# Third batch's k and q also through DMA transposes, two plain heads per row, attention stores on GpSimd's queue

## The chip, the cores and the metric

The kernel runs on one core of one Trainium2 chip. The metric is device time in microseconds (us) of one execution. The kernel before the change takes 313.95 us, the median of 13 runs that lie between 311.17 and 316.79 us.

## The reference

Dilated and plain sliding-window attention on 8 batches, 8 heads, 576 positions and head size 64, then a feed-forward layer with SiLU on the 4608 tokens. Inputs and output are float32; the kernel computes in float16 with float32 accumulation.

```python
scores = scale * np.matmul(q, k.transpose(0, 1, 3, 2))
rel = pos[:, None] - pos[None, :]
mask_plain = (rel >= 0) & (rel < 32)                       # heads 0 to 3
mask_dil = (rel >= 0) & (rel < 128) & (rel % 4 == 0)       # heads 4 to 7
attn = softmax(where(mask, scores, -1e9));  o = attn @ v
x = o.transpose(0, 2, 1, 3).reshape(4608, 512)
h = x @ w_in                                               # 512 x 2048
out = (h * sigmoid(h)) @ w_out                             # 2048 x 512
```

## The kernel before, in words

**Feed-forward.** Tokens go in groups: two of 256, then eight of 512. A group has 16 first-layer tiles `h` (line 892, 4 matmuls each: weights `w_in`, moving operand x transposed, 512 or 256 columns). ScalarE takes the tanh of a tile (line 901) and VectorE makes `gT = (th + 1) * h` of it (line 903). The second layer (line 925) makes an output tile `y` of 128 tokens by 16 matmuls of 512 columns, in four steps of 4; step n reads the n-th quarter of `w_out`. ScalarE copies it out (line 938) and its queue stores it.

**Attention.** Of each batch the first four heads are "plain", the last four "dilated" (positions split in 4 residues). A batch's score work is cut in sets (`S`, lines 605 to 650): matmuls of transposed k and q (line 632), exp on ScalarE, a mask product on VectorE. The products with v (`P` plain, `D` dilated, line 677) are divided by their sums on VectorE (lines 680 and 681) into `oP` and `oD`.

**Two ways to transposed k and q.** Batches below `PEB` (0, 1 and 2) take the PE path: k and q are loaded with positions on partitions (`nat`, `issue_nat`, line 124, GpSimd's queue) and transposed on TensorE against an identity: `TD` for dilated heads (line 544), `TA` and `TB` for plain ones (lines 521 and 535), these after VectorE has put two heads side by side (`paired`, `N`, line 656). The results are copied out of PSUM by VectorE or ScalarE (lines 510 and 512). Batches 3 to 7 take the DMA path: `issue_cast` (line 141) copies k and q to DRAM in float16 (`kq_s`), and `issue_turn` loads them by DMA transposes from SyncE's queue, n = 0 and 1 for plain k and q (line 155, into the `nat` buffers), n = 2 and 3 for dilated k and q (line 158, into `kqT`). The plain transpose reads 2304 rows of 128 elements at a step of 64, so that each row holds a position and the next one.

**Attention's output.** Of batches 0 to 2, `oP` and `oD` are transposed on TensorE into `xA` (`XP`, `XD`). From batch 3 on they are stored to DRAM (`x_s`, lines 696 and 715, SyncE's queue: two stores of `oP`, two of `oD` for each batch) and come back transposed by DMA for each group (line 450, SyncE's queue).

**What sets the order.** The code is written out as one program in which each engine runs its instructions in the order written. At build time a planner (`Plan`, `Step`) picks the next piece of TensorE work from three lists (attention of each batch in an order written out by hand, first-layer tiles, second-layer steps) by estimated costs and due times. The loads of the start are issued in the order of `ORDER` with the costs `LOAD_US`. DMA-path work is written where the planner believes its inputs to be there: `loads_gen(b)` (line 424) first writes "fence" copies on GpSimd, which wait for the dilated transposes of the batch before (line 427) and for the x transpose of an earlier group (line 429), then v's two loads (lines 165 and 178) and the cast of batch b; `turn_gen(b)` (line 410) writes the four transposes; `stored(b)` starts `group_gen` (line 447) once four stores of a batch are written. The number of buffers is two for `nat`, `kqT` and v, three for x in flight.

**The start.** Eight matmuls of 512 columns on zeros (line 192) keep TensorE busy before data is there. Batch 0 has its own, finer transposes (`TD`, `TR`, `TA`, `TS`).

Of the kernel before, what the change touches and what calls it, by code (L numbers as in the profile page):

```python
# [16 lines left out]
def kernel(  # L17
# [32 lines left out]
    PEB = 3  # L50
# [5 lines left out]
    ORDER = "k0 r0 w0b v0 w0a w1 w2 w3 d1 p1 o0 r1 o1 o2 o3 v1".split()  # L56
    LOAD_US = {"w": 2.57, "o": 2.57, "d": 3.2, "p": 3.0, "r": 2.3, "v": 2.57, "k0": 2.2, "r0": 1.0, "v0": 2.3, "w0a": 1.3, "w0b": 1.3}
    AT_W0 = 11.4
# [32 lines left out]
    NW = HN * S  # L91
# [47 lines left out]
    def issue_cast(b):  # L139
        for i, src in enumerate((k, q)):  # L140
            nc.gpsimd.dma_start(
                out=kq_s[b][i].rearrange("(n p c) -> p n c", c=512, p=144),
                in_=src[b].rearrange("h s d -> (h s d)").rearrange("(n p c) -> p n c", c=512, p=144),
            )

    def issue_turn(b, n):
        i = n % 2
        flat = kq_s[b][i]
        if n < 2:
            if b < PEB + 2 and i == 0:  # L150
                nc.gpsimd.memset(kq_plain(b)[0][:, :LEAD], 0.0)
            win = bass.AP(tensor=flat.tensor, offset=flat.offset, ap=[[D, NW], [1, P]])
            dst = kq_plain(b)[i]
            dst = dst[:, LEAD:] if i == 0 else dst
            nc.sync.dma_start_transpose(out=dst[:, None, :], in_=win)
        else:
            rows = flat[HN * S * D :].rearrange("(n c) -> n c", c=DIL * D)
            nc.sync.dma_start_transpose(out=kqTs[b % 2][:, i], in_=rows)
# [29 lines left out]
    warm = vraws[1].rearrange("p a h r d -> p (a h r d)")  # L188
    nc.vector.memset(warm[:, :GT], 0.0)
    y_warm = ps_y.tile([P, GT], F32, tag="y", name="y_warm")  # L190
    for n in range(8):
        nc.tensor.matmul(y_warm, warm[:, :P], warm[:, :GT], start=True, stop=True)
    nc.vector.memset(warm[:, GT:], 0.0)
# [67 lines left out]
    def third_batch():  # L261
        for n in range(2, PEB):
            issue_nat(n, 0, H)
        issue_vraw(2)
        issue_vp(2)
        issue_cast(PEB)
        yield "DMA", 0.0
# [12 lines left out]
    class Plan:  # L280
        def __init__(self):
            self.t = 0.0
            self.now = 0.0
            self.mode = 128
            self.free = {"ACT": 5.7, "DVE": 6.6}
            self.heap = []
            self.n = 0
            self.rings = {nm: [] for nm in RINGS}
# [72 lines left out]
    AT_DIL = {0: 6.1, 1: AT["d1"], 2: t2 + 7.0}  # L361
    AT_PLAIN = {0: 9.3, 1: AT["p1"], 2: t2 + 7.0}
    AT_VRAW = {0: 10.1, 1: AT["r1"], 2: t2 + 8.6}
    AT_VP = {0: 11.4, 1: AT["v1"], 2: t2 + 11.4}
    AT_CAST = t2 + 18.0
# [37 lines left out]
    turned = {b: Step(None, 0.0) for b in range(PEB, B)}  # L403
# [6 lines left out]
    def turn_gen(b):  # L410
        for n, us in enumerate((3.0, 3.0, 1.5, 7.5)):
            issue_turn(b, n)
            yield "DMA", us
        for n in (b, b + 1) if b == 3 == PEB else (b + 1,):
            if n < B:
                count(("L", n), loads_need(n), lambda n=n: start_loads(n))
# [4 lines left out]
    def start_turn(b):  # L421
        plan.push(turned[b], turn_gen(b), plan.now)

    def loads_gen(b):
        last = max(b - 1, PEB)
        for i in range(2):
            nc.gpsimd.tensor_copy(fence[:, i : i + 1], kqTs[last % 2][:, i, 1, HN * M - 1 :])  # L427
        if b - 2 >= PEX:
            nc.gpsimd.tensor_copy(fence[:, 2:3], x_of(first_of[b - 2])[:, HP - 1, GT - 1 :])
        issue_vraw(b)  # L430
        issue_vp(b)
        if b > PEB:
            issue_cast(b)
        yield "DMA", 9.0
        v_in[b].done = plan.now
        if b > PEB:
            yield "DMA", 4.5
            count(("T", b), 2, lambda: start_turn(b))
# [8 lines left out]
    def group_gen(g):  # L447
        t0 = max(GROUPS[g][0], PEX * S)
        n = sum(GROUPS[g]) - t0
        nc.sync.dma_start_transpose(  # L450
            out=x_of(g)[:, :, GT - n :], in_=x_s[t0 : t0 + n]
        )
        yield "DMA", 6.0
        b = need[g]
        if g == first_of[b] and b + 2 < B:
            count(("L", b + 2), loads_need(b + 2), lambda: start_loads(b + 2))

# [8 lines left out]
    def attention(b):  # L466
# [21 lines left out]
        def k_plain(i, hp, j):  # L488
            r = slice(i * D, i * D + D)
            if pe_path:  # L490
                return kP[r, hp, QB * j : QB * j + P]
            c = LEAD + (2 * hp + i) * S + QB * j - W - i
            return kW[r, c : c + P]

        def q_plain(i, hp, j):
            r = slice(i * D, i * D + D)
            if pe_path:
                return qP[r, hp, QB * j : QB * (j + 1)]
            c = (2 * hp + i) * S + QB * j - i
            return qW[r, c : c + QB]  # L500
# [184 lines left out]
        def av_p(ring, j):  # L685
            def lhs(i):
                return prob_cols(("p", j, i // 2), i % 2)

            yield from av(
                ring, f"p{j}", oP[:, j], rcps[:, j], lhs, lambda i: vp[:, i * NB + j, : D + 1]  # L690
            )
            parts[j // 3] += 1
            if not pe_x and parts[j // 3] == 3:
                j = j // 3 * 3 + 2
                rows = x_s[b * S : (b + 1) * S, : HN * D].rearrange("(j p) c -> p j c", p=QB)
                nc.sync.dma_start(
                    out=rows[:, j - 2 : j + 1],
                    in_=oP[:, j - 2 : j + 1].rearrange("p j h d -> p j (h d)"),
                )
                yield "DMA", 3.0  # L700
                stored(b)

        def av_d(ring, ab, r):
# [8 lines left out]
            if not pe_x and parts[2 + ab] == DIL:  # L712
                t0 = b * S + ab * DIL * MH
                rows = x_s[t0 : t0 + DIL * MH, HN * D :].rearrange("(m r) c -> m r c", r=DIL)
                nc.sync.dma_start(out=rows, in_=oD[:, ab].rearrange("p r h d -> p r (h d)"))
                yield "DMA", 3.0
                stored(b)
# [24 lines left out]
        if b == 0:  # L742
            order = [
                ("TA", 1, "q"), ("TA", 0, "q"), ("V", 0), ("TD", 3), ("TS", 1), ("TS", 0),
                ("TD", 0), ("TA", 0, "k"), ("TD", 2), ("TD", 1), ("TA", 1, "k"), ("S", 3),
                ("TR",), ("S", 4), ("S", 6), ("S", 0), ("S", 1), ("D", 0, 1), ("P", 1), ("S", 5),
                ("D", 0, 0), ("D", 0, 2), ("V", 1), ("P", 0), ("S", 2), ("P", 3), ("P", 2),
                ("D", 1, 1), ("P", 4), ("D", 0, 3), ("P", 5), ("XP", 0), ("XP", 1), ("D", 1, 2),
                ("XD", 0), ("D", 1, 0), ("XP", 4), ("D", 1, 3), ("XP", 5), ("XP", 2), ("XD", 1),
                ("XP", 3), ("M",), ("B",),  # L750
            ]
        elif pe_path:
            order = [
                ("N", "k"), ("TD", 3), ("TD", 0), ("TD", 2), ("V", 0), ("TD", 1), ("N", "rest"),
                ("TA", 1), ("N", "q"), ("S", 3), ("TA", 0), ("TB", 0), ("TB", 1), ("D", 0, 1),
                ("D", 0, 0), ("S", 4), ("D", 0, 2), ("S", 0), ("P", 1), ("S", 1), ("D", 0, 3),
                ("P", 2), ("P", 0), ("XP", 0), ("XP", 1), ("S", 5), ("S", 6), ("XD", 0), ("V", 1),
                ("D", 1, 3), ("XP", 2), ("S", 2), ("D", 1, 2), ("D", 1, 0), ("D", 1, 1), ("P", 3),
                ("XP", 3), ("P", 4), ("XD", 1), ("P", 5), ("XP", 4), ("XP", 5),
            ]  # L760
        else:
            order = [
                ("S", 2), ("S", 0), ("P", 1), ("S", 3), ("S", 4), ("S", 1), ("S", 5), ("P", 0),
                ("V", 0), ("P", 5), ("P", 3), ("D", 0, 3), ("V", 1), ("P", 4), ("P", 2),
                ("D", 1, 1), ("D", 1, 3), ("D", 0, 1), ("D", 0, 2), ("D", 1, 2), ("D", 1, 0),
                ("D", 0, 0),
            ]
            if pe_x:
                order.insert(order.index(("D", 0, 0)), ("XP", 0))
                order.insert(order.index(("D", 0, 0)), ("XP", 1))  # L770
                order.insert(order.index(("D", 0, 2)), ("XP", 2))
                order.insert(order.index(("D", 0, 2)), ("XP", 3))
                order.insert(order.index(("D", 1, 0)), ("XP", 4))
                order.insert(order.index(("D", 1, 0)), ("XP", 5))
                order += [("XD", 0), ("XD", 1)]
        for key in order:
# [9 lines left out]
            elif kind == "TA" and b == 0:  # L786
                st = Step(
                    lambda ring, a=a: trans_a0(ring, *a), 0.36, rings,
                    [AT_PLAIN[0]],
# [18 lines left out]
            elif kind == "S":  # L808
                if not pe_path:
                    deps = [turned[b]]  # L810
# [170 lines left out]
    LOOK = 8  # L981
    LIM_ATT = 1.1
    LIM_PAIR = 0.4
    LIM_L1 = 1.8
    SIDE = 0.9
    NEAR = 1.0
    SPARE = 6
    seconds = {st.mate for _, st in att if st.mate}
    side = 0.0
    while att or l1 or l2:  # L990
# [12 lines left out]
        if l2:  # L1003
            main.append((l2, l2[0], 9.0))
        cands = main + cands if side > SIDE else cands + main
# [21 lines left out]
        if pick is None:  # L1027
            waits += [plan.heap[0][0]] if plan.heap else []
# [39 lines left out]
```

The softmax here doesn't subtract the row's maximum and nothing guards it: scores larger than these inputs give would overflow.

## Time and profile before

| what | value |
|---|---|
| median of 13 runs (lowest, highest) | 313.95 us (311.17, 316.79) |
| the profiled execution's own time | 311.17 us |
| its span, first to last instruction | 309.4 us |
| TensorE busy with matmuls | 299.0 us, 97% of the span |
| weight loads, VectorE, ScalarE, GpSimd | 155.5, 196.2, 164.5, 54.7 us |
| bytes moved by DMA | 44.55 MB in 107382 packets |
| first-layer and second-layer matmuls | 640 and 592 |
| first `h` matmul starts | 22.03 us |
| last attention matmul | 231.3 us |

The page of the profile gives busy time by engine, then the span in 40 slices with the busy share in tenths, then the DMA queues, the chain of work that ended last, groups of instructions by line, and DMA issues. A matmul's end is modelled, and a busy TensorE may still run below its peak; start-to-start times say more. Further answers of the trace give waits, order of time by engine, and sums over stretches of time. In instruction groups the row is: line, engine, operation, out<-in, count, busy us, mean ns, idle before it and what ended that.

### The profile page before, as it was taken

The numbers are of one execution on the slowest core, as the hardware profiler recorded it, in microseconds if no ns is written. First come the engines' busy times: TensorE is split into PE (matmuls) and PEld (weight loads), VectorE is DVE, ScalarE is ACT, GpSimd is POOL, SyncE is SP. The second block draws the span as 40 slices with busy tenths as digits, with TensorE's granted clock in tenths as the row PEclk, the third lists the DMA queues.
The fourth block names the chain that finished last, engine by engine and source line by source line (L and its number), as shares of the span: only waits on it lengthen the run. The fifth ranks groups of instructions, "written<-read, shape, count | busy, mean of one in ns | idle before, by whom it ended". The sixth has DMA issues, their size and how long they took to land.

```text
span 309.4 us, 6177 instructions
## 1 busy us (share of the span) xinstructions
PE 299.0 (97%) x2402; PEld 155.5 (50%) x2402; DVE 196.2 (63%) x498; ACT 164.5 (53%) x318; POOL 54.7 (18%) x86
## 2 busy tenths in 40 slices
PE   7789989999999999999999999999999999999995
PEld 3468755555545544554455444544454444444444
DVE  6399998699868735794589457854794355355000
ACT  7478872667573626454663456436643445455111
POOL 8855723001900005000600050000000000000000
PEclk9999999999999999999999999999999999999999
DMA  8999999998999949999999999974115400000222
GB/s 104 184 199 197 195 190 206 204 190 164 141 193 217 181 124 151 217 185 188 134 212 216 200 144 209 231 157 108 38 56 144 98 36 34 34 34 2 79 91 71
DMA packets 107382, 44.55 MB, mean 144 GB/s; under 512 B 73304, under 2 KB 102872, under 8 KB 107352
## 3 DMA queue, kind: packets, MB, share of 16 engines
q0 software_dynamic: 48528, 19.86, 52.6%
q1 hardware_dynamic: 53496, 14.91, 25.3%
q10 hardware_dynamic: 5328, 9.37, 8.8%
q8 instruction: 19, 0.31, 0.4%
q14 instruction: 11, 0.09, 0.1%
HBM read 39.81 MB, written 18.28 MB: 188 GB/s over the span
## 4 chain that ended last, share of the span: by engine, by line
PE 87%; DVE 5%; ACT 3%; DMA 2%; issue 1%; POOL 1%; ACTq 0%; DVEq 0%; POOLq 0%
PE y L925 40%; PE h L892 37%; PE s L632 3%; PE av_d L677 3%; DMA nat<-in_q_dram 2%; PE av_p L677 2%; DVE probs L650 1%; DVE oD L681 1%; ACT probs L641 1%; ACT ob L938 1%; ACT kqD L510 1%; PE s L620 1%; DVE oP L681 1%; DVE gT L903 1%; POOL nat L131 1%
## 5 line engine op out<-in xcount | busy, mean ns | idle before, releaser
L925 PE MATMUL y<-w_out,gT 128*128 128x512 f16 (+1 forms) x592 | 137.8, 373 | 0.0
L901 ACT ACTIVATE th<-h 128x512 f32<-128x512 f32 (+1 forms) x160 | 88.9, 557 | 78.3 <-PE h L892 68.8
L903 DVE SCALAR_TENSOR_TENSOR gT<-th,h 128x512 f16<-128x512 f32 (+1 forms) x160 | 99.2, 628 | 47.7 <-ACT th L901 47.2
L892 PEld LDWEIGHTS <-w_in 128*128 128x128 f16 x640 | 59.0, 97 | 52.3 <-issue 1.2
L925 PEld LDWEIGHTS <-gT 128*128 128x128 f16 x592 | 55.1, 98 | 57.5
L892 PE MATMUL h<-xR,w_in 128*128 128x512 f16 x320 | 77.6, 379 | 0.0
L892 PE MATMUL h<-xA,w_in 128*128 128x512 f16 (+1 forms) x320 | 62.0, 336 | 0.0
L938 ACT ACTIVATE ob<-y 128x512 f32<-128x512 f32 (+1 forms) x36 | 21.3, 591 | 42.6 <-PE y L925 42.6
L641 ACT ACTIVATE probs<-s 128x768 f16<-128x768 f32 (+2 forms) x32 | 24.7, 772 | 11.8 <-PE s L632 10.0
L677 PEld LDWEIGHTS <-probs 128*128 128x128 f16 x448 | 21.9, 98 | 16.1 <-DVE probs L650 3.0
L681 DVE TENSOR_TENSOR oD<-av_d,rcps 72x256 f16<-72x256 f32 x64 | 26.9, 421 | 2.2
L650 DVE TENSOR_TENSOR probs<-probs,mask_p 128x768 f16<-128x768 f16 x21 | 11.5, 551 | 22.6 <-ACT probs L641 22.6
L681 DVE TENSOR_TENSOR oP<-av_p,rcps 96x256 f16<-96x256 f32 x48 | 20.2, 421 | 1.6
L427 POOL COPY fence<-kqT 128x1 f16<-128x1 f16 x10 | 2.3, 232 | 95.7 <-DMA kqT<-kq_s 95.7
L645 ACT ACTIVATE probs<-s 128x384 f16<-128x384 f32 (+2 forms) x38 | 17.2, 479 | 1.0 <-PE s L632 1.0
L677 PE MATMUL av_d<-vd,probs 128*128 128x65 f16 x256 | 15.2, 194 | 1.3 <-DVE oD L681 0.6
L945 DVE TENSOR_SCALAR ob<-y 128x128 f32<-128x128 f32 x1 | 0.3, 290 | 20.6 <-ACT ob L943 20.6
L677 PE MATMUL av_p<-vp,probs 128*128 128x65 f16 x192 | 12.0, 194 | 0.3
L680 DVE RECIPROCAL rcps<-av_d 72x4 f32<-72x4 f32 x64 | 11.0, 172 | 2.0 <-PE av_d L677 1.9
L165 POOL DMA_DIRECT2D vraw<-in_v_dram x16 | 10.8, 677 | 5.6 <-DVE gT L903 2.2
L650 DVE TENSOR_TENSOR probs<-probs,mask_d 128x576 f16<-128x576 f16 (+1 forms) x23 | 11.6, 512 | 0.0
L680 DVE RECIPROCAL rcps<-av_p 96x4 f32<-96x4 f32 x48 | 8.3, 172 | 5.2 <-PE av_p L677 5.2
(93 smaller groups left out, 155.9 us busy)
## 6 DMA issues: line engine op xcount, KB each, us to landing
out_dram<-ob ACTq DMA_DIRECT2D x35, 256.0 KB, 2.9
kq_s<-in_k_dram POOLq DMA_DIRECT2D x5, 576.0 KB, 8.9
kq_s<-in_q_dram POOLq DMA_DIRECT2D x5, 576.0 KB, 10.9
vp<-in_v_dram POOLq DMA_DIRECT2D x7, 384.0 KB, 7.4
w_out<-in_moe_w_out_dram POOLq DMA_DIRECT2D x4, 512.0 KB, 10.5
vraw<-in_v_dram POOLq DMA_DIRECT2D x8, 224.0 KB, 5.2
w_in<-in_moe_w_in_dram POOLq DMA_DIRECT2D x3, 512.0 KB, 9.6
x_s<-oP SPq DMA_DIRECT2D x10, 144.0 KB, 3.3
```

The lines of the kernel that those rows point to most:

```text
L165: nc.gpsimd.dma_start(out=vraw[p0 : p0 + m1 - m0, ab].rearrange("p h r d -> p h (r d)"), in_=src[m0:m1],)
L641: nc.scalar.activation(p2, both[:, :, :n], AF.Exp, scale=scale)
L645: nc.scalar.activation(p2[:, i], sp[i][:, :n], AF.Exp, scale=scale)
L650: nc.vector.tensor_tensor(p2, p2, mk, ALU.mult)
L677: nc.tensor.matmul(a[:, i, : D + 1], lhs(i), rhs(i), start=True, stop=True)
L680: nc.vector.reciprocal(rcp[:n], a[:n, :, D : D + 1])
L681: nc.vector.tensor_tensor(o, a[:n, :, :D], rcp[:n, :, None].broadcast_to([n, HN, D]), ALU.mult)
L892: nc.tensor.matmul(h[:, :w], w_in16[:, c, f * P : (f + 1) * P], x_g[:, c], start=(c == 0), stop=(c == HP - 1),)
L901: nc.scalar.activation(th[:, :w], h[:, :w], AF.Tanh, scale=0.5)
L903: nc.vector.scalar_tensor_tensor(gTs[g][:, f, :w], th[:, :w], 1.0, h[:, :w], ALU.add, ALU.mult)
L925: nc.tensor.matmul(y, gTs[g][:, f, tb * P : (tb + 1) * P], w_out16[:, f, c0:c1], start=(f == 0), stop=(f == NFF - 1),)
L938: nc.scalar.activation(ob, y, AF.Copy, scale=0.5)
```

## The change

- `PEB` goes from 3 to 2: batch 2 takes the DMA path. Its outputs still go through TensorE (`PEX` stays 3).
- `issue_cast` writes plain heads two by two: DRAM rows of 128 elements with both heads' 64 at one position. For that it issues, for each of k and q, two copies of 1152 runs of 64 elements and one copy of the dilated heads; six DMAs for a batch where there were two.
- `issue_turn` reads 1152 such rows for plain k and for plain q, where there were 2304.
- Stores of `oP` and `oD` go from SyncE's queue to GpSimd's, in the order in which the planner lets them.
- The fence copy on x (line 429) is gone.
- Start loads are reordered: half of batch 1's k and q (`p1`) ahead of `w_in`, `o1` ahead of `o0`; the cast of batch 2 follows instead of its `nat` loads and precedes its v.
- Nine warming matmuls of 512 columns at the start, and up to 18 us of planned time fillers of 128 columns wherever the planner finds nothing to do (80 in the program).
- Attention's hand-written orders, the planner's limits and its estimates are new. Plain and dilated transposes have due times of their own (`turned["p", b]`, `turned["d", b]`).

In the program order that results, TensorE's list loses 48 transposes of batch 2 (24 `TD`, 16 `TA`, 8 `TB`) and gains 1 + 80 warming matmuls. SyncE's list, from batch 4 on, is: two plain transposes of batch b; the x transpose of an earlier group; two dilated ones of batch b (in batches 6 and 7 the x transpose follows the dilated ones). GpSimd's list of a batch: two fences, three v loads, six casts, then four stores of the batch before it.

```diff
-    PEB = 3
+    PEB = 2
-    ORDER = "k0 r0 w0b v0 w0a w1 w2 w3 d1 p1 o0 r1 o1 o2 o3 v1".split()
+    ORDER = "k0 v0 r0 p1 w1 w0a w0b w2 w3 d1 r1 o1 o0 o2 o3 v1".split()
-    NW = HN * S
+    NW = HP // 2 * S
...
     def issue_cast(b):
         for i, src in enumerate((k, q)):
+            flat = kq_s[b][i]
+            for hp in range(HP // 2):
+                nc.gpsimd.dma_start(
+                    out=flat[hp * S * P : (hp + 1) * S * P].rearrange("(s i d) -> s i d", i=2, d=D),
+                    in_=src[b, 2 * hp : 2 * hp + 2].rearrange("i s d -> s i d"),
+                )
             nc.gpsimd.dma_start(
-                out=kq_s[b][i].rearrange("(n p c) -> p n c", c=512, p=144),
-                in_=src[b].rearrange("h s d -> (h s d)").rearrange("(n p c) -> p n c", c=512, p=144),
+                out=flat[HN * S * D :].rearrange("(n p c) -> p n c", c=512, p=144),
+                in_=src[b, HN:].rearrange("h s d -> (h s d)").rearrange("(n p c) -> p n c", c=512, p=144),
             )
...
-            win = bass.AP(tensor=flat.tensor, offset=flat.offset, ap=[[D, NW], [1, P]])
+            win = flat[: NW * P].rearrange("(n c) -> n c", c=P)
...
-    for n in range(8):
-        nc.tensor.matmul(y_warm, warm[:, :P], warm[:, :GT], start=True, stop=True)
+    for n in range(9):
+        nc.tensor.matmul(y_warm, warm[:, :P], warm, start=True, stop=True)
...
         for n in range(2, PEB):
             issue_nat(n, 0, H)
+        issue_cast(PEB)
         issue_vraw(2)
         issue_vp(2)
-        issue_cast(PEB)
...
     def turn_gen(b):
-        for n, us in enumerate((3.0, 3.0, 1.5, 7.5)):
+        for n, us in enumerate((1.9, 1.9, 1.8, 1.8)):
+            yield "SP", us
             issue_turn(b, n)
-            yield "DMA", us
+            if n == 2:
+                turned["p", b].done = plan.now
+        yield "DMA", 3.0
...
     def loads_gen(b):
+        yield "POOL", 5.5
         last = max(b - 1, PEB)
         for i in range(2):
             nc.gpsimd.tensor_copy(fence[:, i : i + 1], kqTs[last % 2][:, i, 1, HN * M - 1 :])
-        if b - 2 >= PEX:
-            nc.gpsimd.tensor_copy(fence[:, 2:3], x_of(first_of[b - 2])[:, HP - 1, GT - 1 :])
         issue_vraw(b)
         issue_vp(b)
         if b > PEB:
             issue_cast(b)
...
-            c = LEAD + (2 * hp + i) * S + QB * j - W - i
+            c = LEAD + hp * S + QB * j - W
...
-                nc.sync.dma_start(
-                    out=rows[:, j - 2 : j + 1],
-                    in_=oP[:, j - 2 : j + 1].rearrange("p j h d -> p j (h d)"),
-                )
-                yield "DMA", 3.0
-                stored(b)
+                data = oP[:, j - 2 : j + 1].rearrange("p j h d -> p j (h d)")
+                store(rows[:, j - 2 : j + 1], data)
...
+        def store_gen(rows, data):
+            yield "POOL", 0.8
+            nc.gpsimd.dma_start(out=rows, in_=data)
+            yield "DMA", 2.5
+            stored(b)
...
         if pick is None:
+            if plan.t < WARM:
+                if 5.5 < plan.t:
+                    nc.tensor.matmul(
+                        y_warm[:, :P], warm[:, :P], warm[:, :P], start=True, stop=True
+                    )
+                plan.t += 0.056
+                continue
```

## The prediction

> **What bounds the kernel now.** I read busy shares first, then sums by stretch of time, then the chain, then groups and orders of time for the pieces that change.
>
> ```profile
> PE 299.0 (97%) x2402; PEld 155.5 (50%) x2402; DVE 196.2 (63%) x498; ACT 164.5 (53%) x318; POOL 54.7 (18%) x86
> PE   7789989999999999999999999999999999999995
> DVE  6399998699868735794589457854794355355000
> DMA  8999999998999949999999999974115400000222
> PE 87%; DVE 5%; ACT 3%; DMA 2%; issue 1%; POOL 1%; ACTq 0%; DVEq 0%; POOLq 0%
> ```
>
> TensorE is the bound nearly everywhere. VectorE is as full in slices 3 to 6 (15 to 46 us), and the DMA engines are full until about 205 us: they work ahead. The stretches (us, busy of PE, PEld, DVE, ACT, POOL) say where TensorE still loses time:
>
> ```profile
> 15.00:22.00 7.00, 6.13 (x122) 4.38 (x121) 6.13 (x25) 5.94 (x17) 4.37 (x8) 1.00 1.41 197
> 31.00:46.50 15.50, 14.02 (x207) 10.38 (x206) 14.37 (x42) 12.24 (x31) 8.14 (x11) 1.00 1.45 193
> 46.50:85.00 38.50, 38.40 (x368) 20.78 (x366) 32.36 (x91) 23.18 (x46) 10.60 (x17) 1.00 1.33 181
> 148.00:179.00 31.00, 30.90 (x241) 14.97 (x240) 21.13 (x52) 16.24 (x29) 5.03 (x8) 1.00 1.09 190
> 240.00:306.00 66.00, 66.00 (x321) 31.18 (x319) 21.87 (x32) 26.05 (x44) 0.00 (x0) 1.00 0.16 53
> ```
>
> After 46.5 us only some 0.4 us are idle up to 306; then 3.4 us of copying out. So the time can fall in two ways: less TensorE work, or an earlier arrival at 46.5 us. It can rise if TensorE, whose order is fixed, has to wait for data.
>
> **What the Trainium skill says.** "DMA: Bandwidth & Descriptors", section "Issuing engines are not separate DMA queues": DMAs issued from any engine run on the same 16 DMA engines; another issuer saves only issue time. The trace agrees as far as it goes: SyncE's queue is blocked 5.35 us by two plain transposes (below), which a store behind them waits out. The same page, "Specifications", gives 512 bytes as the least transfer at line rate. In this trace a 128-byte packet (v into SBUF) takes 32 ns, a 512-byte one 60, a 1024-byte one 98: small ones are cheap singly, dear per byte. None goes to DRAM at 128 bytes. "TensorE: Matmul & The Clock Gate", "What's actually happening": the array is at half clock until a window of about 3.4 us was busy, and the window runs free of the kernel. The trace agrees: `TD` takes 279 ns at 5 us and 207 ns in batch 0's later piece. The clock column does not show it.
>
> **The change, part by part.**
>
> *Transposes that go.*
>
> ```profile
> L544 PE MATMUL td<-ident_w,nat 96*128 96x96 f16 x48 | 2.7, 206 | 0.0
> L521 PE MATMUL ta<-ident_w,pair_k 96*128 96x96 f16 x16 | 1.3, 205 | 0.6 <-DVE gT L903 0.5
> L521 PE MATMUL ta<-ident_w,pair_rest 96*128 96x96 f16 x16 | 1.3, 206 | 0.0
> L535 PE MATMUL tb<-ident_w,pair_q 96*128 96x96 f16 x16 | 1.2, 206 | 0.0
> ```
>
> Half of each goes: 24 + 8 + 8 + 8 = 48. Start to start they take 42 to 44 ns (the chain has 12 `td` in 0.53 us), so 2.1 us, all on the path. The copies out of PSUM and the pairing go with them (some 4 us of VectorE, 1 of ScalarE); at 46 to 75 us these are not the bound, so 0.
>
> *The start.* `p1` goes ahead of `w_in`. From landings in the trace, the first transfers (through v's part 2) land by 12.7 us; k0 takes 1.4, v's rest 1.3 and 1.1, `p1` 3.1, `w1` 2.55, half of `w0` 1.3. The first `h` then has its weights at 23.4 us, where it starts now at 22.03. In exchange 24 transposes of batch 1 stand ahead of it. The two orders can be laid side by side at the step where the first output tile reads the last quarter of `w_out`: its landing is 45.1 us now, and the bytes ahead of it are the same, so 45 after. Before, 31.4 us of TensorE work (instructions by their start-to-start times, warming left out) lie ahead of that step, which starts at 46.5 us. After, 30.7 us lie ahead: 10.65 before the first `h`, 20.0 after it, so 43.4 without stalls. VectorE's list from first `gT` to the last of the second group is 15.4 us, TensorE's 16.3: jitter will cost some 2 us, as in 31 to 46.5. I take 45.8. Total work is 290.0 us before and 288.0 after (warming left out), so 258.6 and 257.3 remain. Before: 46.5 + 258.6 + 4.3 for stalls and end = 309.4. After: 45.8 + 257.3 + 4.2 = 307.3, which is 2.1 less. In all I gain what the 48 transposes cost.
>
> *Fillers.* 80 x 56 ns = 4.5 us, twice that at half clock. Cover: in the first 22 us TensorE does 9.4 us of work, and the step above waits for its load anyway. Priced at 0; uncovered, up to 4.5. They also open the clock earlier, at a time that does not depend on luck: now it is shut until about 12 us in the profiled run, and by the skill's window that may be some 3 us later in others, 1 to 2 us lost. I take 0.5 of gain against the median, bounds 0 and 1.5.
>
> *Casts.* A batch takes four more DMAs; each issue on GpSimd takes 0.8 to 1.0 us (0.75 for 512 runs, 1.43 for 3072), so GpSimd is busy 8 us for the loads of a batch, not 4.4. It is idle 20 us in front of each fence: 0. Transfer: 4608 packets of 128 bytes. v's 3072 such packets land in 4.0 us when alone, so 4608 take 6.3 us at the same rate (my value), 18 at the rate of 512-byte packets (768 in 3.0 us), 5 at the best seen. With 576 of 1 KB (3.2) the cast is 9.5 us where it was 5.9.
>
> *Plain transposes.* 1152 rows for 2304: each saves about 1.7 us of SyncE's queue and of the engines, so 3.4 a batch, which pays for the casts.
>
> *Fence and stores.* The cycle now:
>
> ```profile
> 149.02 1.34 POOL L165 DMA_DIRECT2D vraw<-in_v_dram  x2 [0.37 <-issue]
> 151.77 0.80 POOL L141 DMA_DIRECT2D kq_s<-in_k_dram  x1
> 163.82 5.35 SPq L155 DMA_TRANSPOSE nat<-kq_s  x2
> 170.23 1.33 SPq L158 DMA_TRANSPOSE kqT<-kq_s  x1
> 172.59 2.36 SPq L158 DMA_TRANSPOSE kqT<-kq_s  x1
> 177.52 0.19 POOL L427 COPY fence<-kqT 128x1 f16<-128x1 f16 x1 [3.65 <-DMA kqT<-kq_s]
> 179.44 0.19 POOL L429 COPY fence<-xR 128x1 f16<-128x1 f16 x1 [1.73 <-DMA xR<-x_s]
> ```
>
> It is 31 us long: v lands 8.5 us after its issue, the cast 5.9 later, then the queue of SyncE with two stores in between, then 2 us for the x fence. After: v 8.5, cast 9.5 less the part that transposes need not await, transposes 3.4 + 3.4 and about 4 to land: plain q is there 19 us after the loads' issue, dilated q 23.5, the next loads 24.5. TensorE's order asks for batches 24.5, 27, 31, 24.5 and 26 us apart (now about 31). Starting at 48.2 us (v of batch 1 landed), batch 2's plain q is there at 59 us; TensorE comes to it at 63. Going on like this the margins are 4 to 8 us, but for the dilated part of batch 4: on SyncE's queue it stands behind the x transpose that waits for batch 3's stores. These come off VectorE at about 107.5; 0.8 each to issue, 3 to land, 1.4 and 3.3 for the transposes, 2.5 to land: 118.5, wanted at 120.4. The stores are also queued behind the next batch's casts on GpSimd, which are issued some 10 us earlier, and the fence behind the stores waits for transposes that come later still. So 0, with a margin of 2 us; if that cover is gone, the wait is TensorE's.
>
> **The sum.** Profiled time 311.17, of which 309.4 span: -2.1 gives 309.1. That run is the fastest of 13 and the median is 2.8 higher. I put the same difference on the median and 0.5 for the clock: 313.95 - 2.6 = 311.3. What is late next is again TensorE's own work.
>
> **The rivals.**
>
> *Small packets, slower than before.* Each 128-byte run into DRAM costs more than one into SBUF, and each cycle is longer by y. For: nothing in the trace shows one. Against: at 1 KB the two take the same 98 ns. It decides from y = 3 us, when batch 6 (margin 4.7, two cycles from the last reset) is late. At y = 4 (packets two thirds dearer) batches 3, 4, 6 and 7 wait 3.2, 1.2, 1.1 and 2.2 us: 7.7 in all, so 311.3 + 7.7 = 319.
>
> *The start eats the gain.* First `h` at 24 to 25 us, weights late twice more, fillers in the way: the `w_out` step at 47.7. 311.3 + 1.9 = 313.2. For: weights land 1.4 us later. Against: the `w_out` load bounds both orders.
>
> That batch 2 stays on its old path is excluded: its transposes are gone from the program's order.
>
> **How the numbers follow.** A difference under 0.5% (312.4 to 315.5) can't be told from none. Forecast 311.3: chance 0.64, its own range 309.2 to 312.9 (clock 1.5, start +1.5). Small packets 0.20, start 0.16. Faster: 0.9 of the first and a fifth of the start, 0.60. Same 0.18. Slower 0.22. The range reaches to 317.5, into the first rival.
>
> **What would show it.** Right: 24 `td`, no wait of PE on `nat` or `kqT`; packets of 128 bytes near 32 ns in casts; the first `h` at 23 to 24.5 us and the step on `w_out`'s last quarter at 45 to 46.5; 0.4 us idle or less after it. Wrong: PE waits for DMA `kqT<-kq_s` or `nat<-kq_s` (small packets, or the stores' order at batch 4 alone), or h waiting for `w_in` beyond 25 us.

## The result and the profile after

The changed kernel takes 317.55 us, the median of 11 runs (316.44 to 320.25); in the runs beside them the kernel before takes 313.34 (48 runs). The ratio is 1.0138, with a 95% interval of 1.0106 to 1.017: slower by 1.4%, where 0.8% faster was forecast. The profiled run of after is a typical one (317.16 us, span 315.1), that of before one of its fastest (311.17, span 309.4), so the two traces differ by 6 us where the medians differ by 4.2. Ratios below are to runs of the kernel before on the same chip; they leave out runs more than 1.5% above the fastest of their kernel, while medians and counts take in all.

First the page of after: busy time by engine, three rows of its 40 slices, and the chain's shares.

```profile
PE 301.8 (96%) x2435; PEld 157.3 (50%) x2435; DVE 194.1 (62%) x487; ACT 162.6 (52%) x313; POOL 99.3 (32%) x125
PE   7989999959989999999999999999999999999995
DVE  7387988336876883796289768788751553355000
PEclk9997999989999999999999999999999999999999
PE 81%; DMA 9%; DVE 5%; POOL 2%; ACT 1%; issue 1%; ACTq 0%; POOLq 0%
```

Before, no slice of TensorE but the last is under 9 tenths after slice 5 (counted from 0); now slice 8 (63 to 71 us) has a 5, and slice 11 (87 to 95) an 8. The clock, full in every slice before, is 7 in slice 3 and 8 in slice 8. DMA, 2% of the chain before, is 9% of it.

Sums by stretch narrow it down (us, busy of PE, PEld, DVE, ACT, POOL, then the granted clock, DMA, GB/s). First before, then after:

```profile
46.50:63.00 16.50, 16.40 (x158) 9.27 (x157) 12.53 (x38) 8.46 (x19) 2.27 (x4) 1.00 1.52 210
63.00:68.00 5.00, 5.00 (x51) 2.73 (x50) 4.42 (x14) 3.03 (x6) 0.00 (x0) 1.00 1.10 180
68.00:73.00 5.00, 5.00 (x58) 2.79 (x55) 4.58 (x12) 3.75 (x10) 0.00 (x0) 1.00 1.16 163
85.00:90.00 5.00, 5.00 (x56) 2.53 (x56) 2.94 (x5) 3.82 (x7) 0.00 (x0) 1.00 1.89 179
```

```profile
46.50:63.00 16.50, 16.46 (x134) 8.51 (x132) 10.38 (x33) 6.69 (x15) 2.96 (x4) 1.00 1.78 175
63.00:68.00 5.00, 1.08 (x6) 0.41 (x5) 1.09 (x2) 1.08 (x2) 0.00 (x0) 1.00 1.53 153
68.00:73.00 5.00, 5.00 (x31) 2.02 (x29) 2.93 (x6) 2.66 (x5) 3.66 (x6) 0.66 0.63 129
85.00:90.00 5.00, 4.06 (x43) 2.07 (x41) 4.79 (x17) 1.19 (x2) 0.00 (x0) 1.00 1.29 127
```

Between 63 and 68 us TensorE does 1.1 us of work in 5; between 68 and 73 it is busy throughout, but with 31 matmuls for 58 and a granted clock of 0.66, so it does much less than "busy" says; between 85 and 90 it is VectorE that is full (4.79 of 5).

Busy time hides a slow clock, so I also counted progress: the matmuls not yet begun at a time t, each at its start-to-start cost at full clock (0.216 us for 512 columns, and so on), added to t. The sum is the end that TensorE would reach without another loss; its rise is the loss in between.

```
t (us)    46.5    63.0    68.0    73.0    85.0    90.0   140.0   300.0
before   299.6   300.2   300.5   301.0   301.7   301.8   302.8   305.6
after    299.0   299.5   303.6   305.4   305.8   307.5   309.2   311.5
```

After is 0.6 us ahead at 46.5 and 0.7 at 63 us. That lead counts the work still to come, of which after has 2.0 us less, so by 46.5 us it has already given back 1.4. It loses 5.9 us from 63 to 73, where before loses 0.8, and 1.7 from 85 to 90, where before loses 0.1. From 90 to 140 it loses 0.7 more than before; the remaining stretches differ little. What happens at 63 us stands in the orders of time of after. TensorE's, with what it waited for in brackets:

```profile
62.70 1.03 PE L935 MATMUL y<-w_out,gT 128*128 128x512 f16 x4
67.65 1.02 PE L902 MATMUL h<-xA,w_in 128*128 128x512 f16 x4 [3.92 <-DVE gT L913]
68.60 0.70 PE L642 MATMUL s<-nat 64*128 64x96 f16 x16
69.24 1.89 PE L902 MATMUL h<-xA,w_in 128*128 128x512 f16 x4
```

The last row is four matmuls in 1.89 us; the row at 67.65 takes 1.02 for the same four. TensorE waited 3.9 us for a `gT`, whose reading would have made an `h` buffer free. `gT` needs the tanh of line 911, on ScalarE:

```profile
61.18 0.60 ACT L948 ACTIVATE ob<-y 128x512 f32<-128x512 f32 x1 [0.27 <-PE y L935]
65.84 0.34 ACTq L949 DMA_DIRECT2D out_dram<-ob  x1
66.28 1.08 ACT L911 ACTIVATE th<-h 128x512 f32<-128x512 f32 x2 [4.50 <-DMA nat<-kq_s]
```

ScalarE copied an output tile out, then stood 4.5 us at issuing its store (ACTq) before it took up two tanh that were waiting. What released it is the landing of `nat<-kq_s`, the transpose of batch 2's plain q, with which an output store has nothing to do. The built program says why the two are tied: in it, DMAs of SyncE's and ScalarE's queues are given one of eight semaphores in turn, in the order written, and a store that takes over the semaphore of the DMA eight places before it waits until that one has landed. For this, the third output store, that DMA is the transpose. The issues of SyncE's queue, and then their time to landing (issues between 46 and 66 us, last column):

```profile
50.90 6.50 SPq L161 DMA_TRANSPOSE nat<-kq_s  x2
57.45 8.16 SPq L164 DMA_TRANSPOSE kqT<-kq_s  x2
```

```profile
vp<-in_v_dram POOLq DMA_DIRECT2D x1, 384.0 KB, 17.7
...
nat<-kq_s SPq DMA_TRANSPOSE x2, 11.1
kqT<-kq_s SPq DMA_TRANSPOSE x2, 8.4
```

The two plain transposes are issued at 50.9 and 54.9 and land 11.5 and 10.8 us later, at 62.4 and 65.8, in a stretch in which v of the same batch and the end of its cast are still on the way.

### The profile page after: what moved, and what is told of

The parts are those of the page before. It is cut to its first block, busy times and chain, and to the rows that moved or that the text cites. A ratio compares the mean times of both kernels' runs of the same rounds, so it can differ in the third digit from the quotient of the medians.

```text
span 315.1 us, 6249 instructions
## 1 busy us (share of the span) xinstructions
PE 301.8 (96%) x2435; PEld 157.3 (50%) x2435; DVE 194.1 (62%) x487; ACT 162.6 (52%) x313; POOL 99.3 (32%) x125
## 4 chain that ended last, share of the span: by engine, by line
PE 81%; DMA 9%; DVE 5%; POOL 2%; ACT 1%; issue 1%; ACTq 0%; POOLq 0%
PE y L935 37%; PE h L902 36%; DMA nat<-kq_s 3%; PE s L642 3%; DVE gT L913 3%; DMA vp<-in_v_dram 3%; DMA w_in<-in_moe_w_in_dram 2%; PE av_d L687 2%; PE av_p L687 2%; POOL nat L131 1%; DVE oD L691 1%; DVE vd L522 1%; DMA out_dram<-ob 1%; ACT th L911 1%; POOL vp L188 0%
## 5 line engine op out<-in xcount | busy, mean ns | idle before, releaser
L935 PE MATMUL y<-w_out,gT 128*128 128x512 f16 (+1 forms) x592 | 139.5, 374 | 0.2 <-DVE gT L913 0.2
L911 ACT ACTIVATE th<-h 128x512 f32<-128x512 f32 (+1 forms) x160 | 87.8, 556 | 83.6 <-PE h L902 72.8
L902 PEld LDWEIGHTS <-w_in 128*128 128x128 f16 x640 | 60.3, 99 | 61.2 <-issue 6.6
L902 PE MATMUL h<-xA,w_in 128*128 128x512 f16 (+1 forms) x320 | 64.3, 345 | 4.8 <-DVE gT L913 4.1
L651 ACT ACTIVATE probs<-s 128x768 f16<-128x768 f32 (+2 forms) x30 | 23.6, 787 | 11.3 <-PE s L642 10.7
L143 POOL DMA_DIRECT2D kq_s<-in_q_dram x12 | 22.6, 2592 | 0.6 <-DMA w_out<-in_moe_w_out_dram 0.6
L725 POOL DMA_DIRECT2D x_s<-oD x10 | 7.5, 762 | 39.5 <-DVE rcps L690 39.5
L655 ACT ACTIVATE probs<-s 128x384 f16<-128x384 f32 (+2 forms) x40 | 18.7, 479 | 1.7 <-ACT ob L948 1.7
L143 POOL DMA_DIRECT2D kq_s<-in_k_dram x12 | 16.4, 1659 | 0.0
L147 POOL DMA_DIRECT2D kq_s<-in_q_dram x6 | 15.7, 2615 | 1.2 <-DMA w_out<-in_moe_w_out_dram 1.2
L725 POOL DMA_DIRECT2D x_s<-oP x10 | 11.6, 1163 | 13.3 <-DVE oP L691 13.0
```

Source lines behind the costliest of these rows:

```text
L143: nc.gpsimd.dma_start(out=flat[hp * S * P : (hp + 1) * S * P].rearrange("(s i d) -> s i d", i=2, d=D), in_=src[b, 2 * hp : 2 * hp + 2].rea ...
L147: nc.gpsimd.dma_start(out=flat[HN * S * D :].rearrange("(n p c) -> p n c", c=512, p=144), in_=src[b, HN:].rearrange("h s d -> (h s d)").re ...
L651: nc.scalar.activation(p2, both[:, :, :n], AF.Exp, scale=scale)
L655: nc.scalar.activation(p2[:, i], sp[i][:, :n], AF.Exp, scale=scale)
L725: nc.gpsimd.dma_start(out=rows, in_=data)
L902: nc.tensor.matmul(h[:, :w], w_in16[:, c, f * P : (f + 1) * P], x_g[:, c], start=(c == 0), stop=(c == HP - 1),)
```

## The experiments

Two theories came from the trace. **A**: the loss is ScalarE's store, held by a semaphore that it shares with a late transpose. **B**: batch 2's scores ask for k and q before these have landed, and taking the store away would only show that wait. Rivals were C, the stores on GpSimd's queue, and the small packets of the prediction. The order in which an engine's instructions are written is the same in the changed kernel and in the kernels of "Three tiny loads" and "v before the cast", but for what each names.

**Three tiny loads** on SyncE's queue, and a memset of their tile on VectorE, ahead of batch 3's transposes. These then stand behind the third output store in the turn of the eight semaphores. The store becomes the eighth such DMA of the program, has none eight places before it, and so waits for no earlier one.

```diff
+        if b == 3 and n == 0:
+            nc.vector.memset(tiny, 0.0)
+            for m in range(3):
+                nc.sync.dma_start(out=tiny[:, m], in_=v[0, 0, :P, :4])
```

> The changed kernel with three tiny loads (16 bytes a partition) on SyncE's queue ahead of batch 3's transposes, and a VectorE memset of their tile. They shift which earlier DMA a store of ScalarE's queue has to wait for: the third output store no longer follows the plain q transpose of batch 2. Theory A (ScalarE's queue is blocked by that store, which waits for the landing of a transpose issued eight DMAs earlier, and the 4.1 us wait of TensorE at 63 us and the 3.4 us of half clock after it come from there): the store is issued at about 62 us, both go, 317.5 falls to 312 to 313.5; some 1 us remains since the transposes themselves land at 65.8. Theory B (TensorE waits for batch 2's transposes, whoever else waits too): the wait moves to the first scores that read them, 316 to 317.5.

Measured: 314.9 us (20 runs), ratio to before 1.0042 (1.0011 to 1.0074). ScalarE's order of time in this kernel:

```profile
61.11 0.60 ACT L954 ACTIVATE ob<-y 128x512 f32<-128x512 f32 x1 [0.27 <-PE y L941]
61.74 0.34 ACTq L955 DMA_DIRECT2D out_dram<-ob  x1
62.18 1.25 ACT L917 ACTIVATE th<-h 128x512 f32<-128x512 f32 x2 [0.47 <-PE h L908]
```

The store goes out at once. The transpose is as late as before (plain q lands at 66.4), and now the scores wait for it:

```profile
PE s L648 <- DMA nat<-kq_s: 2.6, 3, 1.9
```

A is right: with the semaphore out of the way the ratio falls by 0.0096, some 3.0 us. Of B a wait of 1.9 us is left, after which no half clock follows. The edit has a side effect. The memset stands at 86.9 us in VectorE's list, and the tiny loads wait for it, so batch 3's transposes go out at 88.5 us, not at 79.4 as in the changed kernel:

```profile
87.04 1.31 SPq L159 DMA_DIRECT2D tiny<-in_v_dram  x3
88.51 2.65 SPq L167 DMA_TRANSPOSE nat<-kq_s  x2
```

So the 3.0 us are what the edit brings in all, with what that delay may cost.

**Batch 2 back on the PE path in the changed kernel.**

```diff
-    PEB = 2
+    PEB = 3
```

> The changed kernel with PEB back at 3, so that batch 2 is transposed on TensorE again; all else of the change stays (two heads side by side, stores on GpSimd's queue, fillers, load order). The output stores then have no young transpose eight DMAs before them at 63 us. Theory A or B (the loss is made by batch 2's move): 2.1 us of transposes come back and 5.8 us of waiting and half clock go, 313 to 314.5. Rival C (the loss comes from stores on GpSimd or from the start): 317 to 320.

Measured: 330.52 us (4 runs), ratio 1.0522 (1.0462 to 1.0583). No theory expected that. The orders and due times of the changed kernel are made for the other path; batch 2's v now stands behind its `nat` loads as well as a cast, now that of batch 3, and VectorE stops for it:

```profile
68.28 0.76 DVE L522 COPY vd<-vraw 128x1024 f16<-128x1024 f16 x2 [5.58 <-DMA vraw<-in_v_dram]
```

TensorE waits 4.7 us for what is queued behind it there, and 4.8 us for an x transpose at 129 us. It tells nothing of the PE path by itself.

**The pair layout alone**, put into the kernel before: pairwise casts (line 143) and 1152-row transposes, nothing else.

```diff
-    NW = HN * S
+    NW = HP // 2 * S
...
-            win = bass.AP(tensor=flat.tensor, offset=flat.offset, ap=[[D, NW], [1, P]])
+            win = flat[: NW * P].rearrange("(n c) -> n c", c=P)
```

> The kernel before with the pair layout alone: casts that write two plain heads side by side, plain transposes of 1152 rows, and the indices of the scores. Engine orders and planner estimates stay. The small packets' rival: each batch's data later by 3 us or more, waits at the scores of batches 5 and 6 (margins 1.6 us), 315 to 320. Theory A (128-byte packets cost 32 ns in DRAM too): nothing to be seen, 312.5 to 314.

Measured: 313.45 us (20 runs), ratio 0.9996 (0.9966 to 1.0025). As theory A of this expectation said, in the order of the kernel before small packets cost nothing that shows, and shorter transposes bring nothing.

**The stores of attention back on SyncE's queue.**

```diff
-            yield "POOL", 0.8
-            nc.gpsimd.dma_start(out=rows, in_=data)
+            yield "SP", 0.8
+            nc.sync.dma_start(out=rows, in_=data)
```

> The changed kernel with the attention stores back on SyncE's queue (and planned there). Batch 2's part of the program is as in the changed kernel: the third output store still follows the plain q transpose. Theory A and B: the wait at 63 us stays, 316.5 to 319. Rival C (stores in GpSimd's queue hold up loads or fences): 312 to 315.

Measured: 320.31 us (4 runs), ratio 1.0178 (1.0097 to 1.026). Most runs lie above the 316.5 to 319 that A and B expected. ScalarE is held again, for 5.4 us where it was 4.5:

```profile
65.75 0.34 ACTq L949 DMA_DIRECT2D out_dram<-ob  x1
66.19 1.08 ACT L911 ACTIVATE th<-h 128x512 f32<-128x512 f32 x2 [5.39 <-DMA nat<-kq_s]
```

C is out as the cause of the loss. In the changed kernel GpSimd issues the first of these stores long after the wait at 63 us and the stretch of 85 to 90:

```profile
113.92 1.47 POOL L725 DMA_DIRECT2D x_s<-oD  x2 [10.78 <-DVE rcps L690]
```

The Trainium skill, "DMA: Bandwidth & Descriptors", section "Issuing engines are not separate DMA queues", says that another issuer gives no other DMA engines. This run is in keeping with it, since the other issuer brings no gain, but does not test it by itself.

**v before the cast.** The kernel with the tiny loads, in which v of batch 2 is issued ahead of batch 2's cast, not behind it. (The expectation's first sentence is garbled; this is the edit.)

```diff
-        issue_cast(PEB)
         issue_vraw(2)
         issue_vp(2)
+        issue_cast(PEB)
```

> This kernel is e1_lanes with v's loads of batch 2 written ahead of its cast instead of before batch 3's only in name: of batch 2, v goes first, then the cast, and the planner's plan stays as it is. It tells what the 1.9 us wait of the first scores of batch 2 (plain q landing at 66.4 us in e1_lanes) is made of. Theory B (the transposes are late because the DMA engines still have v's 3072 and 1152 packets to move when the transposes start): with v out of the way the transpose, though issued about 4 us later, needs 5 us instead of 11 to land, plain q is there at 63 to 65 us, the wait falls from 1.9 to under 0.7 us, time 313 to 314. Rival D (the DMA engines simply have more to move by 66 us than they can, in whichever order): plain q lands at 66 us again or later, the wait stays at 1.5 us or more, time 314.5 to 316.

Measured: 313.54 us (12 runs), ratio 1.0005 (0.9966 to 1.0044): the kernel before's time. With the tiny loads alone the plain transposes go out at 51.2 and 55.3 and land at 63.1 and 66.4. Now they go out 4.4 us later, at 55.6 and 59.7, and still land earlier, at 62.4 and 63.3, after 6.8 and 3.7 us. With fewer transfers beside them (batch 3's, issued at 86.0 and 87.4 us in this kernel) such transposes take 3.3:

```profile
nat<-kq_s SPq DMA_TRANSPOSE x2, 3.3
```

So they are not slow by themselves: v's transfers on the same DMA engines made plain q 3 us later. Rival D, which had plain q at 66 us again, is out. But the order is not all. Plain k lands no earlier than in the changed kernel (62.4 in both), and plain q still 4.3 us after the 59 of the forecast: now the cast, which has to land first, comes behind v. What is left is at batch 4, the place where the prediction saw a margin of 2 us:

```profile
PE h L908 <- DMA xA<-x_s: 1.8, 1, 1.8
...
PE s L648 <- DMA kqT<-kq_s: 0.5, 1, 0.5
```

How much of this comes from the tiny loads is open: they hold batch 3's transposes to 86.0 us, and the loads of batch 4 wait for those.

**Batch 2's scores due later**, in the changed kernel, and then together with the tiny loads.

```diff
-    AT_CAST = t2 + 8.5
+    AT_CAST = t2 + 13.0
```

> The changed kernel with one number different: batch 2's scores are due 4.5 us of TensorE work later, so that first-layer tiles and second-layer steps stand where they stood. Plain q of batch 2 lands at about 66 us, and is asked for at about 67. Theory A (ScalarE's third output store waits for the plain transpose issued eight hardware-queue DMAs before it, and stops the tanh behind it): this wait stays, since the store and the transposes are where they were; TensorE runs dry again at 63 to 67 us for 3 to 4 us on h behind gT, with 3.4 us of half clock after it; time 316 to 317.5. Rival B alone (what costs the time is that batch 2's scores come before their data): the waits at 63 to 68 us are gone, time 312 to 313.5.

> Both at once: three tiny loads ahead of batch 3's first transpose, so that the third output store no longer stands eight behind a transpose of batch 2, and batch 2's scores due 4.5 us later. If A and B together are the loss between 63 and 73 us, no wait of TensorE over 0.5 us is left between 60 and 75 us, and the time is 2 us below e1_lanes: 312 to 313.3, equal to the kernel before or up to 0.4% faster. If 314 or more, a third loss is there (VectorE as the bound near 90 us, worth 1.6 us; or the first output stores).

Measured: 327.1 us (4 runs), ratio 1.034 (1.0237 to 1.0442), and 323.56 us (4 runs), ratio 1.0317 (1.0247 to 1.0388). Both totals lie far above what was expected; the stretch in question is as expected. The four kernels between 60 and 75 us, in this order: changed kernel, tiny loads alone, due time alone, both.

```profile
60.00:75.00 15.00, 11.08 (x69) 4.88 (x67) 6.72 (x14) 5.58 (x11) 5.66 (x9) 0.89 1.29 146
```

```profile
60.00:75.00 15.00, 13.14 (x108) 6.49 (x107) 9.76 (x21) 8.00 (x15) 4.17 (x7) 1.00 1.23 133
```

```profile
60.00:75.00 15.00, 12.61 (x65) 5.35 (x64) 6.17 (x10) 6.25 (x12) 7.32 (x11) 0.89 1.37 155
```

```profile
60.00:75.00 15.00, 15.00 (x97) 7.06 (x95) 10.05 (x21) 9.02 (x17) 4.47 (x7) 1.00 1.21 135
```

Only with both is TensorE busy for all 15 us at full clock. A and B together are the loss between 63 and 73 us. With the due time alone the store still holds ScalarE, until plain q has landed:

```profile
64.57 0.34 ACTq L949 DMA_DIRECT2D out_dram<-ob  x1
65.01 1.09 ACT L911 ACTIVATE th<-h 128x512 f32<-128x512 f32 x2 [2.98 <-DMA nat<-kq_s]
```

The totals are worse because a due time moves everything that the planner places after it. With both edits TensorE meets an x transpose that isn't there, at 188 us:

```profile
PE h L908 <- DMA xR<-x_s: 5.2, 1, 5.2
```

Half clock lasts 6.8 us there, so that some 9 us of progress go between 180 and 200 us.

**More fillers**, 118 for 80, in the changed kernel.

```diff
-    WARM = 18.0
+    WARM = 25.0
```

> The changed kernel with fillers allowed up to 25 us of planned time: 118 instead of 80. In the changed kernel TensorE idles before the first h at 24.8 us and then has 3.4 us at half clock. Theory (the half clock is the price of idling, and of no account for the end, since the last-quarter step of w_out waits for its load at 45 us anyway): the half clock at 24 to 28 us goes or moves, the step stays at 45.5 to 46 us, and the time is 316.5 to 318, no change from the changed kernel. Rival (the start's half clock is carried to the end, 1.7 us): 315 to 316.

Measured: 320.81 us (4 runs, 316.82 to 322.31), ratio 1.0138 (1.0025 to 1.0251): too wide to separate from the changed kernel; the median is above both expectations. The stretch at the start, in the changed kernel and in this one:

```profile
22.00:31.00 9.00, 7.90 (x85) 5.77 (x83) 6.81 (x21) 6.81 (x18) 2.90 (x5) 0.81 1.33 202
```

```profile
22.00:31.00 9.00, 8.22 (x113) 6.86 (x110) 7.30 (x22) 7.24 (x20) 2.67 (x4) 1.00 1.33 202
```

The half clock at 24.4 to 27.8 us is gone, and progress is 1.1 us better at 28 us, 0.4 at 46.5. The step on the last quarter of `w_out` begins at 47.0 us in both. Then the wait at 63 us is 5.6 us long, not 3.9: plain q lands at 66.6 us, 0.8 later, and the half clock there lasts 6.8 us, not 3.4. What the start gains, and more, is lost to the wait for batch 2.

**Batch 4 mended**, on top of v before the cast: the planner is told that stores of batch 3 take longer, writes batch 4's dilated transposes ahead of the x transpose, and asks for batch 3's x 4.3 us of work later. The second kernel has the 118 fillers too.

```diff
-            yield "DMA", 2.5
+            yield "DMA", 6.5 if b == 3 else 2.5
```

> e5_v_first with one estimate changed: a store of batch 3 is put down as taking 6.5 us to land instead of 2.5. The planner then writes batch 4's dilated transposes ahead of the x transpose on SyncE's queue, and asks for batch 3's x 4.3 us of TensorE work later. Theory (what e5_v_first still loses between 119 and 140 us, 2.6 us of progress, is its 1.8 us wait on that x transpose, which waits for stores that take 7 us to land beside transposes and casts, with a spell of half clock after it): the wait is gone, the time 310.8 to 312, some 0.7% faster than before. Rival (the batches after it, whose order moves as well, pay it back on a later transpose, as the later due time did near 155 and 192 us): a wait over 1 us after 150 us, 313 to 316.

> e10_x3 with fillers allowed up to 25 us of planned time, 118 instead of 80. In e8_warm25 this removed the spell of half clock at 24.8 to 28 us and left 0.4 us of it at 46.5 us, but its later wait at 63 us was longer and hid that. If the start is worth what progress at 46.5 us says: 0.4 us below e10_x3. If the w_out step hides all of it: equal to e10_x3 within 0.3 us. If fillers cost: 0.5 us or more above.

Measured: 314.85 us (21 runs, 312.59 to 317.37), ratio 1.0057 (1.0025 to 1.0088), and 316.94 us (6 runs), ratio 1.0146 (1.0094 to 1.0199). The theory's first half held, its time (310.8 to 312) did not: between 119 and 140 us TensorE is busy 20.57 of 21 us, where the kernel with v first has 18.72; the half clock that the expectation names there was not in the trace of either. But the time did not fall. In the profiled run the start, in the same written order as with v first, happens to have no half clock. TensorE is 0.6 us further at 63 us and waits for batch 2:

```profile
64.61 0.52 PE L648 MATMUL s<-nat 64*128 64x96 f16 x16 [1.43 <-DMA nat<-kq_s]
```

More goes between 140 and 160 us: 1.7 us of progress, where the kernel with v first loses 0.4 and the kernel before 0.8. With more fillers three such waits for `nat` add up to 6.5 us (63, 91 and 118 us). No version here beats the kernel before. Not measured: v first without the tiny loads, and batch 2's scores 2 us later on top of the mended batch 4.

## Why the prediction was wrong

**The step that failed** is "Fence and stores", in its sentence "Starting at 48.2 us (v of batch 1 landed), batch 2's plain q is there at 59 us; TensorE comes to it at 63", and so "margins are 4 to 8 us" and "So 0". Plain q landed at 65.8 us. The transpose was issued at 54.9, which the forecast's 59 less 4 gives too. The term that was mis-sized is "about 4 to land": it was 11. I had priced the transposes as in a steady cycle, v, then cast, then transposes, one after the other; at batch 2 the cast is issued first and v last, so that v's transfers lie on top of the transposes. The skill's sentence on DMA engines that all issuers share stood in the prediction, for the stores; it was not put to use for this stretch. v before the cast shows it: 6.8 and 3.7 us to land. Even so plain q comes at 63.3, not 59, so part of the error is the traffic as a whole and no matter of order. As a price of the steady cycle the 19 us held roughly: in after, plain q of batches 4 to 7 lands 18 to 22 us after the first load of v is issued. And the profile of before had a warning for the stretch in question. Two of its loads issued between 34 and 50 us, the last column being the time to landing:

```profile
kq_s<-in_k_dram POOLq DMA_DIRECT2D x1, 576.0 KB, 15.2
nat<-in_q_dram POOLq DMA_DIRECT2D x1, 384.0 KB, 17.2
```

The same cast takes 8.9 us in the median of that kernel. The Trainium skill, "Perfetto Trace Analysis", section "DMA Instruction — HWDGE (DVE, Sync)", warns that a DMA's bar ends when its descriptors are handed over and leaves the transfer out. The trace agrees: the two bars of the plain transposes take 2.2 us on average, the landings 11.1. The time has to be read from landings in a stretch that is as full as the one predicted.

**A wait that I didn't consider** came on top. The change puts four transposes of batch 2 on SyncE's queue ahead of the first output stores, and by the turn of eight semaphores the third store waits for one. The prediction asked what stands behind a waiting instruction on SyncE and GpSimd, but says nothing of ScalarE's queue. The tiny loads alone bring the ratio from 1.0138 to 1.0042.

**Half clock after the wait** is part of this. The Trainium skill, "TensorE: Matmul & The Clock Gate", section "What's actually happening", has the gate closed after an idle window of about 3.4 us. In after, half clock follows the wait of 3.9 us and lasts from 68.8 to 72.2, 3.41 us, which costs 1.7; after waits of 1.8 and 1.9 us (v first, tiny loads) it doesn't come. But the traces also show half clock after less idling than that: with the later due time alone a wait of 2.4 us is followed by 3.41 us of it (67.7 to 71.1), and at the start of after it comes at 24.4 us, though TensorE was busy for 2.2 of the 3.4 us before, with no wait over 0.7. Here the measurement decides: in these traces a wholly idle window is not needed, and the length of one wait does not settle it.

**The start was priced too early as well.** First `h` came at 24.8 us, outside "23 to 24.5", with half clock from 24.4 to 27.8. The step on the last quarter of `w_out` began at 47.0 us, outside "45 to 46.5" and 1.2 after the forecast's 45.8. By the prediction's own sum after should lead by 2.0 us at this step (46.5 + 258.6 against 45.8 + 257.3); the table above has 0.6 at 46.5. So the rival in which the start eats the gain came true in large part (it had the step at 47.7), beside the loss at batch 2. The loss is not the same in every execution: in the profile of the kernel with batch 4 mended, whose written order up to there differs only in v and the cast of batch 2, no half clock comes, first `h` starts at 23.4 and the step at 45.5, as forecast. One profile of each kernel does not tell how often.

**Right were** the 48 transposes (work counted from the trace: 2.0 us less) and the casts' packets: 128 bytes into DRAM take 32 ns, as those into SBUF, and the layout alone gives 0.9996. GpSimd's busy time is 99.3 us, not 54.7, and after the start the waits show no more than 0.4 us of an engine for GpSimd. The margin of 2 us at batch 4 was named, with its mechanism; in the kernel with v first, where TensorE arrives nearly on time, it is overrun by 1.8 us, with the tiny loads as a possible part of the cause.

**What the sum lacks.** As a share of the kernel before's time the forecast is 0.9916 and the result 1.0138, some 7.0 us apart. The tiny loads take away 3.0 of that, v before the cast 1.2 more (here the intervals overlap). Some 2.8 us are left. By the trace of the kernel with v first, the start (some 0.8 us short of the forecast at 46.5 us), the x wait at batch 4 and a stretch at 80 to 85 us are in it. In the last of these batch 2's products with v are bunched and VectorE, which divides each, is busy 4.73 of 5 us; it is the stretch of 85 to 90 in after. No run moved that bunch, so its share is argued, not shown. Why mending batch 4 brought nothing in the median stays open too: its profiled run (313.15) is among its faster ones, so its trace may not show what the median lost.

## What to carry to other kernels

A batch moved from a path on TensorE to one by DMA arrives when the DMA engines have time; price it from landings under the traffic of that stretch, and order what must land first ahead of what is wanted later. When DMAs are added to a hardware queue, list which later DMA of every such queue takes over their semaphores, since an output store can hold up all that its engine has to compute. When due times feed a planner, change one only with the whole order after it in view. And look where a probe's own instructions come to stand: the tiny loads freed one store and held back four transposes.

## What had not been expected of the hardware

- A transpose of 1152 rows lands in 3.3 us with few other transfers, and in 10.8 to 11.5 us beside a cast and loads of v: a factor of three.
- A wait of 3.9 us on TensorE is followed by one spell of half clock of 3.41 us (clock 0.66 between 68 and 73 us), one of 2.4 us (later due time) by 3.41 too, and waits of 1.8 and 1.9 us by none. Beside waits of 4.8 and 5.6 us (stores back, more fillers) it lasts 6.83 us and begins while TensorE still waits.
- One copy of 1152 runs (line 143) takes GpSimd 1.35 us from the end of the instruction before it to its own end, one copy of the dilated heads 0.71 us, and one of the copies before (line 141) 0.77. The recorded durations are longer, 1.7 us for k and 2.6 us for q on average, because they overlap: the copies start 0.8 us apart. The busy times of such groups therefore count some of it twice.
